# An FFT layer with two MLPs on one core: the first eight steps in written order, GpSimd kept to the squares' low parts

## The chip, the cores and the metric

The kernel runs on one core of a Trainium2 chip. The time is device microseconds of one execution, the median of 3 runs. Below, TensorE is the matmul engine (PE in the profile, PEld its weight loads), VectorE is DVE, ScalarE is ACT, GpSimd is POOL, and SyncE (SP) issues the DMAs.

## The reference

```python
X = np.fft.fft(x, axis=1)            # x is 2 x 3008 x 256
X = np.fft.fft(X, axis=2)
x = X.real.reshape(6016, 256)
h = x @ moe_w_in;  r = np.maximum(h, 0.0);  x = (r * r) @ moe_w_out     # 256 -> 2048 -> 256
h = x @ moe2_w_in; g = h / (1 + np.exp(-1.702 * h)); out = g @ moe2_w_out
```

All inputs are float32.

## The kernel before

Every float32 operand of a large matmul is split into a high part, rounded to the narrower type fp32r, and a low part, the rest; a product is three matmuls (high by high, high by low, low by high). A split costs a cast on ScalarE and a subtraction on another engine. The MLP weights come in as 64-bit words and are narrowed first: passes over 128x1024 that clamp, shift, mask, or and add (`narrow`, L162 to L187); then, for the first matrix, a sum and a difference (L207, L208), the cast (L210) and the subtraction of the low part (L78, the helper `sub`). `widen` yields these passes one by one for a weight group, named (mlp, kind, g); a step's f is the number of a slice of 128 of the 2048 hidden columns, and group g holds slices 4g to 4g+3.

The run has three stretches.

- The start: the first batch's three tiles of x (q = 0, 1, 2) are folded (`fold`: sums and differences of 128x512 and 128x1024, L281 to L293), multiplied by the feature table (`part`, L317, written to `zc` and `zs`), and summed over positions (`halves`, L361) into block (0, 0). The Nyquist terms come from a small table x128 (`fold_nyquist`, L255 to L262).
- 128 steps. Step i takes block j and slice f: `front1` is 6 matmuls into a PSUM tile pair `psa` (L462 to L464), of which there are two; VectorE makes three passes from it (L805, L807, L808: p, then the two halves of h); ScalarE relu, square and cast to the high part `gh` (L814, L815, L817); the low part `gl` is a subtraction (L78) made one step later, on GpSimd, or on VectorE in the steps of `VSTEPS`. `back` is 12 matmuls of step i - 4 (L477) into `psb`. A block's steps use weight group 0, later ones groups 1, 2, 3; step 20 is the first with group 2.
- 48 units of the second MLP (from about 480 us), in an order written by hand.

Other work of the steps (narrowing the other weights, the other blocks of batch 0, batch 1's folds) is background: `PLAN` names for each job the step where it begins, its passes per step, and the step by which it must be done; `background(i)` runs them after each step's own code. Outside the hand-written part a scheduler with its own costs and priorities sets each engine's order; from step 18 (`THROTTLE`) on, a step's background may not be issued ahead of the step's last VectorE and ScalarE instruction.

Of the kernel before, what the change touches and what calls it, by code (L numbers as in the profile page):

```python
# [16 lines left out]
P = 128  # L17
# [35 lines left out]
NP2 = 512
# [12 lines left out]
def spectral_two_mlps_kernel(  # L66
# [78 lines left out]
    x128_t = small.tile([P, 6, 8], F32, name="x128_t")  # L145
    nc.sync.dma_start(x128_t, x128)
# [3 lines left out]
    w1n_raw = small.tile([P, 32], U32, name="w1n_raw")  # L150
    nc.sync.dma_start(w1n_raw, w1n.bitcast(U32))
# [70 lines left out]
    def widen_in(g, ue, dests, then=None):  # L222
# [9 lines left out]
        for o, x, y, op in ((s3, a11, a21, ALU.subtract), (a21, a21, a22, ALU.add), (s2, a21, a11, ALU.subtract),  # L232
                            (s4, a12, s2, ALU.subtract)):
            yield lambda: G.tensor_tensor(out=o, in0=x, in1=y, op=op)
        for r in range(2):
# [7 lines left out]
            yield lambda: [sub(G, l, x, o) for o, l, x in parts]  # L243
# [22 lines left out]
    V.memset(still, 0.0)  # L266

    def keep_busy(o, k):

        for _ in range(k):  # L270
            last = T.matmul(o, lhsT=still, rhs=still, start=True, stop=True, skip_group_check=True)
        return last


    def fold(q, then=None):
        b, c = divmod(q, NC)
# [12 lines left out]
        gv = g.rearrange("p r (i j) s -> p r i j s", j=2)  # L289
        u = xt[:, 1, 0:4].rearrange("p (r j) s -> p r j s", r=2)  # L290
# [3 lines left out]
        if b == 0:  # L294

            slots = [[(u, 0, 0), (u, 1, 0)], [(u, 0, 0), (u, 1, 1)], *([(gv[:, :, j], 0, 0), (gv[:, :, j], 1, 1)] for j in range(2))]
        else:
# [3 lines left out]
            slots = [[(fu, 0, 0)], [(fu, 1, 0)], [(fv, 0, 0)], [(fv, 1, 0)]]  # L301
        if then:
            then()
        if c == 0:
            zc[b] = zp.tile([P, NC, 4, 130], F32, tag="zc", name="zc")
            zs[b] = zp.tile([P, NC, 4, P], F32, tag="zs", name="zs")

        def part(par):

            ps = ps_b() if b == 0 and par else ps_a()  # L310
            cols = slice(0, 130) if par == 0 else slice(130, 258)
            if par == 0 and q in WARM:
                keep_busy(ps[:, 0, 384:512], WARM[q])
            for s in range(4):
                o = ps[:, s // 2, (s % 2) * 130:(s % 2) * 130 + 130] if par == 0 else ps[:, 0, s * P:(s + 1) * P]
                for i, (v, j, minus) in enumerate(slots[s]):
                    T.matmul(o, lhsT=v[:, par, j], rhs=dft[:, minus, cols],  # L317
                             start=(i == 0 and (s % 2 == 0 if par == 0 else s == 0)), stop=(i == len(slots[s]) - 1),
                             skip_group_check=True)
            return ps  # L320

        def even():
            pc = part(0)
            for s in range(4 if q < 2 else 0):
# [769 lines left out]
```

## Time and profile before

| what | value |
|---|---|
| median of 3 runs | 976.22 us (975.21 to 976.83) |
| the profiled execution | 974.99 us |
| its span, first to last instruction | 973.2 us |
| mean granted TensorE clock | 0.998 of full |

The span is 1.8 us shorter than the execution's own time. Busy times of an engine are the union of its instructions; an engine off the path may be idle without cost.

### The profile page before, as it was taken

Reading aid. Unit: us, or ns where it says so; the run is one execution under the profiler, and the core shown is the slowest. Engines: PE = TensorE matmul, PEld = TensorE weight load, DVE = VectorE, ACT = ScalarE, POOL = GpSimd, SP = SyncE. Lnnn points to the kernel's source line nnn. Section 1 sums busy time; section 2 is a strip of 40 time slices with the busy share of each in tenths; the row PEclk is TensorE's granted clock in tenths of the full one; section 3 lists DMA queues with packets and bytes.
Section 4 is the critical chain, followed back from the end, with each engine's and each line's share of the span. In section 5 each row is a group of like instructions: output and inputs, shape, how many; then the busy total and the mean of one; then the engine's idle time right before and its main releaser. Section 6 shows DMA issues by size and latency. Waiting matters only on the chain.

```text
span 973.2 us, 12586 instructions
## 1 busy us (share of the span) xinstructions
PE 954.7 (98%) x4872; PEld 852.9 (88%) x4872; DVE 699.6 (72%) x870; ACT 599.6 (62%) x700; POOL 329.3 (34%) x203
## 2 busy tenths in 40 slices
PE   9899999999999999999999999999999999999998
PEld 9579989898999799999888888888888888888996
DVE  6995798985879688996689855566575476556653
ACT  3589878765676678778785644554455354445442
POOL 5358677633585457756403220020002002000000
PEclk9999999999999999999999999999999999999999
DMA  7541232311011001100131020010011002000001
GB/s 303 208 148 64 76 133 93 137 35 57 9 67 44 33 1 47 67 6 33 51 112 44 1 87 0 1 65 22 1 44 43 1 1 82 1 1 10 34 1 39
DMA packets 21899, 53.58 MB, mean 55 GB/s; under 512 B 3280, under 2 KB 15184, under 8 KB 19152
## 3 DMA queue, kind: packets, MB, share of 16 engines
q1 hardware_dynamic: 21840, 52.79, 15.4%
q8 instruction: 38, 0.62, 0.3%
q14 instruction: 21, 0.17, 0.1%
HBM read 37.36 MB, written 15.42 MB: 54 GB/s over the span
## 4 chain that ended last, share of the span: by engine, by line
PE 76%; DVE 5%; ACT 3%; issue 1%; DVEq 0%; ACTq 0%
PE psb L872 26%; PE psc L856 23%; PE psb L477 17%; PE psa L462 3%; PE psa L464 3%; PE psa L463 3%; PE psa L361 1%; ACT h L815 1%; ACT h L814 1%; ACT gh L817 1%; DVE h L807 1%; DVE p L805 0%; DVE h L808 0%; PE psa L317 0%; DVE ue L185 0%
## 5 line engine op out<-in xcount | busy, mean ns | idle before, releaser
L78 POOL TENSOR_TENSOR gl<-h,gh 128x752 fp32r<-128x752 f32 (+1 forms) x118 | 223.2, 1897 | 152.5 <-ACT gh L817 108.6
L477 PE MATMUL psb<-gh,w 128*128 128x376 f32 (+1 forms) x1024 | 237.3, 335 | 0.2 <-ACT h L814 0.2
L477 PEld LDWEIGHTS psb<-gh,w 128*128 128x128 f32 x1024 | 182.6, 188 | 0.7 <-ACT h L814 0.4
L872 PE MATMUL psb<-gh,w 128*128 128x512 f32 (+1 forms) x576 | 163.7, 386 | 0.0
L936 DVE TENSOR_TENSOR g<-u,psc 128x1024 f32<-128x1024 f32 (+1 forms) x48 | 57.6, 1201 | 115.4 <-PE psc L856 115.4
L814 ACT ACTIVATE h<-h 128x752 f32<-128x752 f32 (+1 forms) x114 | 94.8, 833 | 58.1 <-DVE h L808 48.0
L477 PE MATMUL psb<-gl,w 128*128 128x376 f32 (+1 forms) x512 | 130.1, 335 | 0.0
L938 ACT ACTIVATE g<-g 128x1536 f32<-128x1536 f32 (+1 forms) x48 | 70.4, 1467 | 95.1 <-DVE g L936 95.1
L872 PEld LDWEIGHTS psb<-gh,w 128*128 128x128 f32 x576 | 108.1, 188 | 20.6
L817 ACT CAST gh<-h 128x752 fp32r<-128x752 f32 (+1 forms) x128 | 105.1, 822 | 31.8 <-DVE h L812 28.5
L78 DVE TENSOR_TENSOR gl<-g,gh 128x2048 fp32r<-128x2048 f32 (+1 forms) x48 | 109.5, 2282 | 1.2 <-ACT gh L913 1.2
L638 POOL TENSOR_TENSOR ue<-raw 128x512 f32<-128x512 f32 (+1 forms) x10 | 21.5, 2165 | 255.0 <-DMA raw<-ydram 173.6
L805 DVE SCALAR_TENSOR_TENSOR p<-n,w1n_t,psa 128x376 f32<-128x376 f32 (+1 forms) x128 | 76.5, 600 | 43.3 <-PE psa L464 43.1
L815 ACT ACTIVATE h<-h 128x752 f32<-128x752 f32 (+1 forms) x114 | 95.2, 836 | 3.1
L462 PE MATMUL psa<-eo,w 128*128 128x376 f32 (+1 forms) x256 | 88.1, 345 | 5.0 <-DVE h L808 2.7
L477 PEld LDWEIGHTS psb<-gl,w 128*128 128x128 f32 x512 | 92.6, 188 | 0.0
L913 ACT CAST gh<-g 128x2048 fp32r<-128x2048 f32 (+1 forms) x48 | 90.3, 1881 | 0.1
L872 PE MATMUL psb<-gl,w 128*128 128x512 f32 (+1 forms) x288 | 87.7, 386 | 0.0
L463 PE MATMUL psa<-eo,w 128*128 128x376 f32 (+1 forms) x256 | 85.8, 335 | 0.0
L464 PE MATMUL psa<-eo,w 128*128 128x376 f32 (+1 forms) x256 | 85.6, 334 | 0.0
L807 DVE TENSOR_TENSOR h<-p,psa 128x376 f32<-128x376 f32 (+1 forms) x128 | 69.7, 545 | 13.9 <-POOL gl L78 1.0
L935 ACT ACTIVATE g<-psc 128x512 f32<-128x512 f32 (+1 forms) x48 | 28.3, 590 | 76.0 <-PE psc L856 76.0
(151 smaller groups left out, 1551.1 us busy)
## 6 DMA issues: line engine op xcount, KB each, us to landing
ydram<-o SPq DMA_DIRECT2D x17, 376.0 KB, 2.9
xt<-in_x SPq DMA_DIRECT2D x5, 1024.0 KB, 7.0
out<-o SPq DMA_DIRECT2D x10, 512.0 KB, 2.6
cst<-in_dfts SPq DMA_DIRECT2D x8, 570.0 KB, 5.2
raw<-in_w1i SPq DMA_DIRECT2D x4, 1024.0 KB, 4.9
raw<-in_w1o SPq DMA_DIRECT2D x4, 1024.0 KB, 5.8
raw<-in_w2i SPq DMA_DIRECT2D x4, 1024.0 KB, 4.9
raw<-in_w2o SPq DMA_DIRECT2D x4, 1024.0 KB, 4.9
```

The lines of the kernel that those rows point to most:

```text
L78: eng.tensor_tensor(out=o, in0=a, in1=f32(b), op=ALU.subtract)
L462: T.matmul(o, lhsT=w[:, 0, fs], rhs=t[:, par, 0, 0:wd], start=True, stop=False)
L463: T.matmul(o, lhsT=w[:, 0, fs], rhs=t[:, par, 1, 0:wd], start=False, stop=False)
L464: T.matmul(o, lhsT=w[:, 1, fs], rhs=t[:, par, 0, 0:wd], start=False, stop=True)
L477: T.matmul(acc[j][ec][:, s, 0:wd], lhsT=w[:, hl, e0:e0 + P], rhs=(gh, gl)[gi][:, s, 0:wd], start=(first and hl == 0 and gi == 0), stop=(la ...
L807: V.tensor_tensor(out=h[:, 0, 0:wd], in0=p[:, 0:wd], in1=ps[:, 1, 0:wd], op=ALU.add)
L814: A.activation(out=hv, in_=hv, func=AF.Relu)
L815: A.activation(out=hv, in_=hv, func=AF.Square)
L817: last_a = A.copy(gh[:, :, 0:wd], hv)
L856: T.matmul(bank, lhsT=w[:, hl, slot * P:(slot + 1) * P], rhs=x[:, yl, 0:wd], start=(first and hl == 0 and yl == 0), stop=(hl == 1), skip_g ...
L872: T.matmul(o[:, s, 0:wd], lhsT=w[:, hl, e0:e0 + P], rhs=g[:, 2 * i + s, 0:wd], start=(f == 0 and hl == 0 and g is gh), stop=(f == 15 and h ...
L913: A.copy(gh, gs[u - 1])
```

## The change

The start is no longer left to the scheduler: from the first load to the end of step 7 the order of every engine is as the code is written (`HAND = 8`). In detail:

- VectorE makes all folds and the Nyquist terms, which stand first in its order; GpSimd made half of the differences and the Nyquist terms. The loads of x128 and of the small weight table stand ahead of the feature table's.
- The first tile needs one fold pass fewer and 12 matmuls a part where it had 8. 24 warm-up matmuls on zeros stand ahead of it where there were 36; the groups of 3 and of 5 in the first steps are gone.
- Block (0, 1)'s sums stand ahead of step 0's front; they stood between step 0's front matmuls. Their evacuation and the narrowing of (0, 1, 0) are set into places of steps 0 to 5.
- The narrowing of the other weights of the first MLP (`conv`) begins at step 5; it began at step 3, free of the throttle until step 18. The throttle now begins at step 8.
- All low parts of weights and of blocks, and the sums of the second MLP's first groups, go to VectorE; `VSTEPS` is empty, so that GpSimd makes every `gl`.
- From step 8 on `gl` of step i is made in step i + 2, and waits for the last of VectorE's narrowing passes in the background of step i + 1; the first VectorE pass of a step stands behind that last pass in VectorE's order.

```diff
 PLAN = {
-    "out0": (0, 12, 3), "even01": (0, 1, 4), "odd0": (1, 1, 48), "conv": (3, 1.2, 36),
+    "odd0": (6, 1, 48), "conv": (5, 1.2, 36),
-WARM = {0: 36, 2: 4, "first": 3, "second": 5}
-THROTTLE = 18
+WARM = {0: 24, 2: 2}
+HAND = 8
+THROTTLE = HAND
...
-VSTEPS = {44, 45, 50, 69, 71, 79, 82, 99, 101, 109}
+VSTEPS = set()
-EOG = {1, 2, 3}
+EOG = set()
...
     load_x(0)
+    x128_t = small.tile([P, 6, 8], F32, name="x128_t")
+    nc.sync.dma_start(x128_t, x128)
+    w1n_raw = small.tile([P, 32], U32, name="w1n_raw")
+    nc.sync.dma_start(w1n_raw, w1n.bitcast(U32))
     dft = zp.tile([P, 2, 258], F32, tag="dft", name="dft")
...
-            yield lambda: G.tensor_tensor(out=o, in0=x, in1=y, op=op)
+            yield lambda: V.tensor_tensor(out=o, in0=x, in1=y, op=op)
...
+        z_tiles(0)
+        fold_nyquist()
+        run(fold_rows(0))
+        z_even(0, part(0, 0))
+        run(fold_rows(1))
+        z_odd(0, part(0, 1))
+        w_abs()
+        z_even(1, part(1, 0))
+        run(fold_rows(2))
+        w_low()
+        z_odd(1, part(1, 1))
...
+        put(0, "front", copy, o_low, adds)
+        put(0, "V", high)
+        put(1, "front", nyquist)
+        put(1, "V", n_copy1, low)
+        put(1, "A", n_adds1, o_shift)
+        put(2, "front", next_of(odd))
+        put(2, "V", next_of(odd), o_or, o_add)
+        put(2, "A", lambda: load_w(0, 1, 1), out_high)
+        put(3, "front", next_of(odd))
...
+    def behind_tail(x, sync):
+        kind = mybir.DependencyClass.Sync if sync else mybir.DependencyClass.NoSync
+        tc.add_manual_dep(x.ins, tail[0].name, mybir.DependencyInfo(kind, mybir.DependencyReason.DATA), reason="tail")
...
     def background(i):
+        tail[0] = last_v.ins
...
-            if not run(entry[2], int((i + 1) * entry[1]) - int(i * entry[1])):
+            before = len(traced())
+            more = run(entry[2], int((i + 1) * entry[1]) - int(i * entry[1]))
+            if entry[0] in NARROW:
+                of_v = [x for x in traced()[before:] if x.engine == last_v.ins.engine]
+                if of_v:
+                    tail[0] = of_v[-1]
...
+        if i > THROTTLE:
+            behind_tail(first_v, False)
...
-        if pend:
-            low_part(*pend)
-        pend = (i, (j, f), h, gh)
+        do_early(i, "A")
+        pend.append((i, (j, f), h, gh))
+        if len(pend) > (1 if i < THROTTLE else 2):
+            low = low_part(*pend.pop(0))
+            if low is not None and i > THROTTLE:
+                behind_tail(low, True)
```

Three places show what moves. VectorE at the start of the program, before (`t`, `xt` are fold tiles, `ne`, `nu` and `nyq` the Nyquist terms):

```order
L266 MEMSET still 128x128
L283 TENSOR_TENSOR t<-xt 128x512 x2
L287 TENSOR_TENSOR xt<-t 128x512
L288 TENSOR_TENSOR xt<-t 128x512
L293 TENSOR_TENSOR xt<-xt 128x512
L281 TENSOR_TENSOR t<-xt 128x512
```

The same place of VectorE in the changed kernel:

```order
L265 MEMSET still 128x128
L255 TENSOR_TENSOR ne<-x_t 128x24
L257 TENSOR_TENSOR nyq<-ne 128x6x2
L258 TENSOR_TENSOR nu<-ne 128x12
L259 TENSOR_TENSOR nyq<-nu 128x6
L260 TENSOR_TENSOR nyq<-nu 128x6
L261 TENSOR_SCALAR nyq<-nyq 128x24
L281 TENSOR_TENSOR t<-xt 128x512
L282 TENSOR_TENSOR t<-xt 128x512
L281 TENSOR_TENSOR t<-xt 128x512
L282 TENSOR_TENSOR t<-xt 128x512
L286 TENSOR_TENSOR xt<-t 128x512
```

Six Nyquist passes and two differences have come in ahead of the first tile's last fold.

TensorE around step 0's front before (L361 with `cst` are the block sums, L462 to L464 the front):

```order
L361 MATMUL psa<-cst,zs 128x188 x2
L462 MATMUL psa<-eo,w 128x378 x2
L361 MATMUL psa<-cst,zc 128x188 x2
L361 MATMUL psa<-cst,zs 128x188 x2
L463 MATMUL psa<-eo,w 128x378
L464 MATMUL psa<-eo,w 128x378
```

And in the changed kernel (the front is L480 to L482):

```order
L369 MATMUL psb<-cst,zc 128x189 x4
L369 MATMUL psb<-cst,zc 128x188 x4
L369 MATMUL psb<-cst,zs 128x188 x4
L480 MATMUL psa<-eo,w 128x378
L481 MATMUL psa<-eo,w 128x378
L482 MATMUL psa<-eo,w 128x378
```

Block (0, 1)'s sums now stand whole ahead of the first front matmul.

The low part of weight group (0, 0, 2) before, on GpSimd (here w_894; h_517, h_558, h_594 and h_626 are the squares of steps 4, 5, 6 and 7):

```order
L78 TENSOR_TENSOR gl_567<-h_517,gh_524 128x2x376
L207 TENSOR_TENSOR ue_809<-ue_809 128x512
L78 TENSOR_TENSOR gl_603<-h_558,gh_565 128x2x376
L78 TENSOR_TENSOR gl_642<-h_594,gh_601 128x2x376
L78 TENSOR_TENSOR w_894<-ue_809,w_894 128x1024
L78 TENSOR_TENSOR gl_662<-h_626,gh_640 128x2x376
```

The same group in the changed kernel, on VectorE (w_972; p_996 is of step 18, p_1028 of step 19, p_1058 of step 20; L755 is a copy out of a block's sums):

```order
L208 SCALAR_TENSOR_TENSOR ue_868<-ue_868,mask_122 128x512
L959 SCALAR_TENSOR_TENSOR p_996<-n_397,w1n_t_123,psa_975 128x376
L963 TENSOR_TENSOR h_995<-p_996,psa_976 128x376
L964 TENSOR_TENSOR h_995<-p_996,psa_976 128x376
L959 SCALAR_TENSOR_TENSOR p_1028<-n_397,w1n_t_123,psa_1007 128x376
L963 TENSOR_TENSOR h_1027<-p_1028,psa_1008 128x376
L964 TENSOR_TENSOR h_1027<-p_1028,psa_1008 128x376
L755 COPY o_1036<-psb_796 128x2x376
L80 TENSOR_TENSOR w_972<-ue_868,w_972 128x1024
L959 SCALAR_TENSOR_TENSOR p_1058<-n_397,w1n_t_123,psa_1049 128x376
```

It has moved from between the low parts of steps 6 and 7 to just ahead of step 20's first pass, and step 20 is the first that uses it.

## Rows read from the trace of the kernel before

**Rows 1.** The page, part 1: busy time by engine.
```profile
PE 954.7 (98%) x4872; PEld 852.9 (88%) x4872; DVE 699.6 (72%) x870; ACT 599.6 (62%) x700; POOL 329.3 (34%) x203
```
**Rows 2.** Busy time by stretch: length, engines (instructions), clock, DMA share, GB/s.
```profile
31.60:79.30 47.70, 43.12 (x211) 34.29 (x211) 43.33 (x62) 36.86 (x49) 28.55 (x14) 0.96 0.44 162
79.30:110.00 30.70, 30.70 (x180) 30.70 (x179) 19.86 (x33) 26.22 (x34) 20.14 (x12) 1.00 0.11 39
110.00:185.20 75.20, 70.56 (x399) 67.40 (x399) 67.96 (x99) 59.95 (x75) 51.49 (x28) 1.00 0.36 119
185.20:480.00 294.80, 294.22 (x1695) 285.76 (x1694) 234.48 (x346) 214.27 (x272) 172.75 (x103) 1.00 0.11 38
```
**Rows 3.** Busy time by stretch: the clock's fall and return, and a steady stretch.
```profile
47.50:50.20 2.70, 0.29 (x1) 0.00 (x0) 2.70 (x5) 0.84 (x1) 2.70 (x2) 1.00 0.69 291
50.20:53.60 3.40, 3.27 (x6) 1.67 (x8) 3.40 (x5) 1.75 (x3) 0.75 (x1) 0.50 0.01 2
...
250.00:300.00 50.00, 50.00 (x291) 50.00 (x291) 42.12 (x60) 37.31 (x47) 33.44 (x22) 1.00 0.11 37
```
**Rows 4.** Timeline of TensorE's start: start us, us, instruction, [idle before <-releaser].
```profile
1.03 10.58 PE L271 MATMUL psa<-still 128*128 128x128 f32 x72 [1.03 <-DVE still L266]
11.46 1.95 PE L317 MATMUL psa<-dft,xt 128*128 128x130 f32 x16
13.24 1.95 PE L317 MATMUL psb<-dft,xt 128*128 128x128 f32 x16
...
24.34 1.33 PE L361 MATMUL psa<-cst,zc 128*128 128x189 f32 x8
...
31.57 0.61 PE L462 MATMUL psa<-eo,w 128*128 128x378 f32 x2
...
39.09 5.34 PE L361 MATMUL psa<-cst,zc 128*128 128x188 f32 x20
...
50.33 4.55 PE L361 MATMUL psa<-cst,zs 128*128 128x376 f32 x12 [2.54 <-DVE ue L420]
```
**Rows 5.** Timeline of TensorE: the first matmul of step 11, and of step 42.
```profile
79.35 0.33 PE L462 MATMUL psa<-eo,w 128*128 128x376 f32 x1
...
185.24 0.33 PE L462 MATMUL psa<-eo,w 128*128 128x376 f32 x1
```
**Rows 6.** Waits of TensorE, 110 to 185 us: us in total, times, longest.
```profile
PE psa L462 <- DVE h L808: 2.0, 5, 1.0
```
**Rows 7.** Lines L805, L176 and L78: ns min/median/max, first and last start.
```profile
L805 DVE SCALAR_TENSOR_TENSOR p<-n,w1n_t,psa x128: 590/599/609, 34.6 to 472.0; 128x376 f32<-128x376 f32 x96, 128x378 f32<-128x378 f32 x32
...
L176 DVE TENSOR_SCALAR ue<-ue x14: 678/695/1924, 21.3 to 512.4; 128x1024 uint32<-128x1024 uint32 x14
...
L78 POOL TENSOR_TENSOR gl<-h,gh x118: 1782/1830/2630, 41.9 to 476.6; 128x752 fp32r<-128x752 f32 x89, 128x756 fp32r<-128x756 f32 x29
```
**Rows 8.** Timeline of SP: the issue of x128's load.
```profile
2.73 0.43 SPq L146 DMA_DIRECT2D x_t<-in_x  x1
```
**Rows 9.** DMA issues: the same load: count, KB, us to landing.
```profile
x_t<-in_x SPq DMA_DIRECT2D x1, 24.0 KB, 5.1
```
**Rows 10.** Timeline of VectorE: folds, a weight's low part, step 16's last two passes.
```profile
6.75 0.69 DVE L283 TENSOR_TENSOR t<-xt 128x512 f32<-128x512 f32 x1 [1.43 <-DMA xt<-in_x]
...
19.92 0.69 DVE L293 TENSOR_TENSOR xt<-xt 128x512 f32<-128x512 f32 x1
...
30.43 1.22 DVE L78 TENSOR_TENSOR w<-ue,w 128x1024 fp32r<-128x1024 f32 x1
...
96.25 0.55 DVE L807 TENSOR_TENSOR h<-p,psa 128x376 f32<-128x376 f32 x1
96.71 0.54 DVE L808 TENSOR_TENSOR h<-p,psa 128x376 f32<-128x376 f32 x1
```
**Rows 11.** Timeline of ScalarE: a weight's cast, a weight's first pass, step 16's relu.
```profile
27.37 1.04 ACT L210 CAST w<-ue 128x1024 fp32r<-128x1024 f32 x1 [2.25 <-DVE ue L208]
...
30.75 1.16 ACT L171 ACTIVATE ue<-raw 128x1024 f32<-128x1024 f32 x1
...
97.28 0.83 ACT L814 ACTIVATE h<-h 128x752 f32<-128x752 f32 x1 [0.45 <-DVE h L808]
```

More of the change, by code (lines that the diff above doesn't have):

```diff
@@ L266, in spectral_two_mlps_kernel, with fold_rows @@
     V.memset(still, 0.0)
+    A.activation(out=w1n_t[:, 0, 0:1], in_=still[:, 0:1], func=AF.Abs)
     def keep_busy(o, k):
         for _ in range(k):
[L271 to L276, printed above, removed]
+            T.matmul(o, lhsT=still, rhs=still, start=True, stop=True, skip_group_check=True)
+    def fold_rows(q):
         xt = xq.pop(q)
         t = xp.tile([P, 2, 8, P], F32, tag="t", name="t", bufs=1)
+        eng = V
         for a in XPARTS[q]:
             yield lambda: (
-                *(e.tensor_tensor(out=t[:, 1, i], in0=xt[:, 0, i], in1=xt[:, 1, i], op=ALU.subtract)
-                  for e, i in (((G, slice(0, 4)), (V, slice(4, 8))) if q in (1, 2) else ((G, a),))),
+                eng.tensor_tensor(out=t[:, 1, a], in0=xt[:, 0, a], in1=xt[:, 1, a], op=ALU.subtract),
                 V.tensor_tensor(out=t[:, 0, a], in0=xt[:, 0, a], in1=xt[:, 1, a], op=ALU.add),
@@ L304, in fold @@
         if c == 0:
[L305 to L324, printed above, removed]
[L325 to L344 removed]
+            z_tiles(b)
+        for par, z in ((0, z_even), (1, z_odd)):
             for _ in range(2 * b):
                 yield lambda: None
[L347 removed]
+            yield lambda: z(q, part(q, par))
     eo, e128 = {}, {}
@@ L429, in nyquist @@
             e128[b, kb] = t
-        yield lambda: sums(0)
-        yield lambda: sums(1)
-        yield lambda: split_eo(b, 2, e2)
+        if b:
+            for par in range(2):
+                yield lambda: (sums(par), leaves(par))
+            yield lambda: split_eo(b, 2, e2)
+        else:
+            for job, par in ((sums, 0), (leaves, 0), (sums, 1), (leaves, 1)):
+                yield lambda: job(par)
+            t = eo[b, 2] = ep.tile([P, 2, 2, NP], F32R, tag="eo", name="eo")
+            yield lambda: A.copy(t[:, :, 0, 0:wd], e2)
+            yield lambda: sub(V, t[:, :, 1, 0:wd], e2, t[:, :, 0, 0:wd])
         yield from [lambda: None] * b
@@ L456, in front1 @@
         pq = ps_a()
-        if at_step[0] == 0 and j == 0:
-            keep_busy(pq[:, 0, 384:512], WARM["first"])
         for par in range(2):
@@ L605, in store @@
             nc.sync.dma_start(y[:, ec, :, 0:wd], o)
-    pend = None
+    pend = []
     n = len(steps)
@@ L789, in spectral_two_mlps_kernel @@
         ps = front1(j, f)
-        if i == 1:
-            o = ps_b()[:, 0, 0:128]
-            for _ in range(WARM["second"]):
-                tc.keep_in_program_order(keep_busy(o, 1))
+        do_early(i, "front")
         done = steps[i - LAG][1:] if i >= LAG else None
```

227 lines of the change are left out of this document (171 added, 56 removed).

## The prediction

> **What bounds the kernel now.** I read the page's busy times first: TensorE is busy for 98% of the span, so only its idle and slow stretches can be won back [rows 1]. The table of stretches says where they are. From 185.2 to 480 us TensorE is busy for 294.22 of 294.80 us: nothing is to be had there, whatever the other engines do [rows 2]. A steady step is 18 matmuls of 376 columns; 291 of them in 50.00 us are 0.172 us each, 3.10 us a step [rows 3]. Two stretches fall short: 31.6 to 79.3 (43.12 of 47.70 us busy, clock 0.96) and 110 to 185.2 (70.56 of 75.20) [rows 2].
>
> The timeline of TensorE gives the first its size. Step 0's front begins at 31.57 us, step 11's at 79.35 [rows 4, 5]: 47.8 us. The work between is 11 fronts of 6 matmuls and 7 backs of 12, 150 x 0.172 = 25.8 us; block (0, 1)'s sums, 16 records at the 1.33 per eight of block (0, 0), 2.7; its Nyquist sums, 8 records, 1.4; the odd blocks' sums, 32 records at 5.34/20, 8.5; a selection of two matmuls, 0.4 [rows 4]. Sum 38.8 us, so 9.0 are lost, to waits (the longest 2.54 us, for VectorE's L420) and to a clock of 0.50 (its level of 1.2 GHz) for the 3.40 us after that wait [rows 3, 4].
>
> For the second, take step 11 to step 42, 79.35 to 185.24: 105.9 us [rows 5]. 31 steps are 96.1; batch 1's first tile (16 records at 0.111, from the 1.78 us between two parts of 16) and a selection are 2.2 [rows 4]. So 7.6 us are lost; the wait named most often is for the step's third pass on VectorE [rows 6].
>
> Why VectorE is late there: a step's three passes read PSUM and keep their time (590 to 609 ns for the first), but L176, which reads SBUF, takes 678 ns at best and 1924 at worst, beside GpSimd's subtractions of 1.83 us [rows 7].
>
> **The change, part by part.** I sum against the profiled execution, 974.99 us. Two passes of 0.55 us start 0.46 apart [rows 10]; I take 0.08 of overlap off each pass.
>
> *To step 0.* VectorE now begins with the Nyquist terms, so it waits for x128. Before, that load was issued at 2.73 us and landed 5.1 later, at 7.8 [rows 8, 9]; now it goes out third, behind x's two halves, the second of which had landed by 6.75 [rows 10]. I take 7.0 (bounds 6.0 to 7.8). The feature table goes out behind two small loads; it is needed only at 12 us: 0. Six small passes: 0.2 each, 1.2 us (not in the trace on this scale; between 0.1 and the 0.55 of larger ones). Six passes of 512 columns at 0.61: the first tile is ready at 12.0, against TensorE's first real matmul at 11.46 [rows 4]. Tiles 1 and 2 cost two long passes (1.2) and three short each, 4.3 us: 16.3 and 20.6. Before, the last fold pass ended at 20.61 with GpSimd's help [rows 10]: folding on VectorE alone costs nothing, as the two engines had slowed each other.
>
> TensorE: 72 warm-up records took until 11.46, about 21 of them at half speed [rows 4]. The new 48 end near 8.8. It then idles for some 3.3 us; the one such wait in the trace, 2.7 us, was followed by the low clock [rows 3]. If so, the next 3.4 us run at half speed and 1.6 us are lost. Then 48 records for tile 0 (5.4), 32 each for tiles 1 and 2 (3.6, and 0.4 of warm-up): 25.0 us at full clock. Block (0, 0)'s sums 2.7, its Nyquist sums 1.4, block (0, 1)'s sums 3.3 (2.7 to 3.9): step 0's front begins at 32.4 at full clock, at 34.0 with the low one, against 31.57. VectorE and ScalarE are ready by 31.1: after the sums a copy (0.5), the weight's cast (1.04), the block's cast (0.8), two low parts (1.2 and 0.9) [rows 10, 11].
>
> *Step 0 to step 11.* Block (0, 1)'s sums now lie ahead, so TensorE has 38.8 - 2.7 = 36.1 us of work. VectorE, from step 0's first pass to step 8's: eight steps of 1.44 us; four passes of 1.14, three of 0.61, four of 0.46, two low parts and a copy of 0.86 each and 0.5 of Nyquist terms, 11.3; and some 2.5 of waits for ScalarE: 25.3 us. TensorE's own work to step 8 is 26.8, so VectorE follows it. Step 11 comes at 32.4 + 36.1 = 68.5, or 70.1 with the low clock, against 79.35: a gain of 10.9 or 9.3. I take 10.0.
>
> *Step 11 to step 42.* Narrowing that ran before step 11 is moved into steps 8 to 33. VectorE's load there is 1.44 us for the step, about 1.15 for narrowing, 0.1 for copies: 2.7 of 3.10. ScalarE's is three passes of 0.83, or 0.75 back to back, and 3.3 us (two first passes, one cast) per weight, 0.7 a step: 2.9 to 3.2 [rows 11]. Both fit, hardly. But a weight's clamp (behind ScalarE's first pass) and its low part (behind the cast) stand ahead of the next step's first pass, so each of ten such places can hold VectorE up. Followed through the order, the two around steps 9 to 13 cost TensorE 2.6 us. Step 20 needs group (0, 0, 2), whose low part now stands just ahead of that step's pass: after step 19's last pass come a relu and a cast (0.83 each), the weight's cast (1.04) and its low part (1.22) [rows 10, 11], and TensorE has two backs, 4.1 us, to fill in: 1.0. The other places: 2.0. Steps 36 to 42, with batch 1's folds: 2.0. Sum 7.6, as much as before: 0. Bounds: 2.5 lost (79.3 to 110 was full [rows 2]) to 15, a gain of 5 or a loss of 7.4.
>
> A rule weighed: beside GpSimd's 1.83 us a VectorE pass grew from 0.68 to 1.92 us [rows 7]. The Trainium skill (SBUF — State Buffer, "SBUF: two separate sides") says that the two engines share one port pair, which one of them holds for a whole instruction. By that the new place of `gl`, beside a step's three passes, isn't free: they last 1.44 us, so the narrowing pass behind them still waits 0.4. Over 25 steps that is 10 us of VectorE, within its slack of 0.4 a step; if all of it fell on the path, the gain would be gone.
>
> *`gl` two steps late.* It starts beside VectorE's first pass of step i + 2 and takes 1.83 us; its matmuls come behind step i + 4's front, 7.2 us after step i + 2's front begins. It is late only if VectorE lags by over 4.6 us; the two `psa` pairs stop TensorE earlier, at 3.7. Queued behind a waiting `gl` on GpSimd are only other `gl`. Cost 0 (-0.5 to 2).
>
> *Rest.* VectorE takes on some 21 us of low parts and folds and gives back ten `gl`. From 185 to 480 us it is busy for 234.48 of 294.80 [rows 2], and the passes lose their collisions: 0.
>
> Sum: 974.99 - 10.0 = 965.0. The median of the runs is 1.23 us above the profiled execution, so I predict 966.2.
>
> **Rivals.**
>
> 1. *The clock stays up and narrowing runs smoothly.* For it: VectorE is freed of the collisions that stretch L176. Against: the idle 3.3 us. Gain 10.9 + 5 = 15.9: 960.3.
>
> 2. *VectorE and ScalarE become the bound in steps 8 to 33* (slower). Place: VectorE's order, where a clamp or low part that waits for ScalarE stands ahead of the next step's p. Where ScalarE lags a full step, such a step lasts relu, square and cast 2.5, a first pass 1.16, two narrowing passes 1.3 and the step's own 1.44: 6.4 us, 3.3 more than TensorE's. Ten places: 33 us. It decides from 1.76 us a place, where 10.0 + 7.6 us are used up. At 3.3 each: 966.2 + 33 - 7.6 = 991.6. For it: ScalarE's 2.9 to 3.2 of 3.10 us. Against: two `psa` pairs let VectorE lag by 3.7 us.
>
> 3. *The start's gain is given back.* TensorE, earlier, meets the narrowing undone: steps 11 to 42 lose 15 us. 966.2 + 7.4 = 973.6.
>
> The Trainium skill (TensorE: Matmul & The Clock Gate, "Part 1") says that an idle array falls to its lower clock by itself. Rows 3 agree; that speaks against rival 1's full gain.
>
> **How the numbers follow.** Forecast (gain 5 to 14) 0.65: 962 to 971. Rival 1 (over 14) 0.10. Rival 3 (gain 2 to 5) 0.10. Within 2 us, about the 0.2% that a measurement of this kernel can tell from no change, 0.06. Rival 2 0.09. Faster 0.85, same 0.06, slower 0.09. The range leaves out part of rival 1 and what lies above a gain of 2: 958.5 to 974.0.
>
> **What would show it.** VectorE's first pass at about 7 us and tile 2's last at 20.6; TensorE's clock at 0.50 after 12 us or not; step 0's front at 32.4 to 34.0, step 11's at 68.5 to 70.1, step 42's 9 to 11 us before 185.24; L176 near 0.7 us. Wrong would be VectorE waiting for ScalarE by over 1.5 us at most of the ten places, TensorE waiting for `gl`, or a stretch from 185 us on that isn't full.

## The result, and the profile after

| | kernel before | changed kernel |
|---|---|---|
| median | 976.53 us (4 runs) | 990.1 us (4 runs, 987.9 to 991.68) |
| ratio, 95% interval | | 1.0137 [1.0118, 1.0155] |
| the profiled execution | 974.99 us | 987.9 us |

The change is slower by 1.4%; the forecast was 966.2 us, 23.9 less. The table of stretches of the changed kernel, with the bounds of [rows 2]; a column is busy time with the count of instructions, then TensorE's granted clock:

```profile
core 0: us, PE busy (x) PEld busy (x) DVE busy (x) ACT busy (x) POOL busy (x), PEclk, DMA share, GB/s
31.60:79.30 47.70, 44.86 (x231) 38.80 (x230) 38.13 (x60) 38.50 (x50) 18.61 (x10) 0.96 0.37 130
79.30:110.00 30.70, 26.84 (x139) 25.03 (x138) 24.51 (x37) 25.80 (x33) 14.57 (x9) 0.94 0.27 94
110.00:185.20 75.20, 64.89 (x338) 59.89 (x338) 58.45 (x87) 53.98 (x66) 36.03 (x19) 0.95 0.26 88
185.20:480.00 294.80, 292.33 (x1684) 283.43 (x1683) 223.06 (x366) 215.13 (x272) 169.42 (x93) 1.00 0.13 44
```

The stretch from 79.3 to 110 us, full before, now lacks 3.9 us, the next one 10.3 where it lacked 4.6. A table by time mixes steps, since the steps have moved. TensorE's timeline gives the fronts of steps 0, 11 and 42 (start, duration, line):

```profile
30.75 0.44 PE L480 MATMUL psa<-eo,w 128*128 128x378 f32 x1
...
67.83 0.34 PE L480 MATMUL psa<-eo,w 128*128 128x376 f32 x1
...
197.27 0.34 PE L480 MATMUL psa<-eo,w 128*128 128x376 f32 x1
```

Against 31.57, 79.35 and 185.24 [rows 4, 5], step 0 is 0.8 us earlier, step 11 is 11.5 earlier and step 42 is 12.0 later. From there on the distance stays between 12 and 14 us. So the start does what was forecast, and steps 11 to 42 lose 23.5 us that the forecast put at 0.

The same steps side by side, first the kernel before, then the changed one:

```profile
0.00:79.35 79.35, 72.53 (x425) 61.06 (x426) 67.26 (x98) 50.10 (x79) 42.35 (x34) 0.98 0.57 212
79.35:185.24 105.89, 101.25 (x577) 98.09 (x577) 87.86 (x130) 86.15 (x108) 71.62 (x40) 1.00 0.29 96
```

```profile
0.00:67.83 67.83, 64.40 (x397) 56.93 (x398) 55.70 (x92) 44.90 (x79) 17.90 (x18) 1.00 0.59 217
67.83:197.27 129.44, 111.41 (x577) 103.02 (x577) 100.58 (x146) 94.60 (x115) 59.24 (x35) 0.95 0.27 93
```

Up to step 11 VectorE does 11.56 us less, and step 11 comes 11.52 us earlier: much of what the start gained is work put off. Five weights had been through VectorE's narrowing by step 11, now three have. It isn't all of it, though: with five weights narrowed again (v3_early, below) the new start still has step 11 3.6 us early, and the old start with only three (y3_before_late) wins just 2.1. Between steps 11 and 42 VectorE does 12.7 us more: some 3.6 are narrowing (five weights in place of three, each in less time), 5.4 the weights' low parts and sums and 3.0 the folds that came from GpSimd. TensorE has the same 577 matmul records there (98.3 us of work by the prediction's count), so VectorE's 100.6 alone is over what TensorE needs. And VectorE waits. The waits of the changed kernel between 68 and 200 us (total, times, longest):

```profile
POOL gl L980 <- DVE w L80: 21.7, 6, 4.7
POOL gl L980 <- DVE ue L176: 16.0, 4, 5.0
DVE w L80 <- ACT w L210: 11.7, 5, 3.6
DVE ue L175 <- ACT ue L171: 10.3, 4, 3.7
PEld psb L495 <- POOL gl L980: 9.2, 10, 2.9
...
PEld psa L480 <- DVE p L959: 6.3, 7, 2.2
```

VectorE stands nine times, 22.0 us in all, behind ScalarE's first pass of a weight (L171) or its cast (L210). Busy and waiting make 122.6 of the 129.4 us: the path runs along VectorE's order, through its own passes and its waits. The same sum holds in all fifteen kernels below, this one included, that have every weight's low part on VectorE: steps 11 to 42 take 107 to 138 us there, 2 to 9 us more than VectorE is busy and waits for ScalarE. One such place, in step 11, from the timelines of ScalarE, VectorE and TensorE (the bracket is the idle time before and what ended it):

```profile
67.63 0.83 ACT L971 ACTIVATE h<-h 128x752 f32<-128x752 f32 x1 [0.35 <-DVE h L964]
68.50 0.83 ACT L972 ACTIVATE h<-h 128x752 f32<-128x752 f32 x1
69.36 0.82 ACT L974 CAST gh<-h 128x752 fp32r<-128x752 f32 x1
70.09 1.04 ACT L210 CAST w<-ue 128x1024 fp32r<-128x1024 f32 x1
...
67.00 0.54 DVE L964 TENSOR_TENSOR h<-p,psa 128x376 f32<-128x376 f32 x1
71.16 1.23 DVE L80 TENSOR_TENSOR w<-ue,w 128x1024 fp32r<-128x1024 f32 x1 [3.62 <-ACT w L210]
72.30 0.60 DVE L959 SCALAR_TENSOR_TENSOR p<-n,w1n_t,psa 128x376 f32<-128x376 f32 x1
...
73.05 0.41 PE L480 MATMUL psa<-eo,w 128*128 128x376 f32 x1 [1.98 <-DVE p L959]
```

ScalarE makes the step's relu, square and cast and only then casts the weight; VectorE does nothing from 67.54 to 71.16, because the weight's low part stands next in its order, ahead of step 10's first pass, whose front was done at 65.9; TensorE, out of free `psa` pairs, stands for 1.98 us, and 1.7 us later its clock falls.

The clock adds to it: it is at 0.50 four times, after pauses of TensorE, where [rows 3] has one such stretch:

```profile
74.80:78.10 3.30, 3.30 (x12) 2.97 (x11) 1.66 (x3) 3.30 (x6) 1.30 (x1) 0.50 0.50 190
105.50:108.80 3.30, 3.30 (x11) 3.30 (x12) 1.07 (x2) 3.30 (x5) 0.32 (x1) 0.50 0.63 233
156.70:160.00 3.30, 3.30 (x11) 3.30 (x12) 3.17 (x5) 2.09 (x3) 0.96 (x1) 0.50 0.45 109
170.40:173.70 3.30, 3.30 (x11) 3.30 (x12) 3.17 (x4) 2.35 (x3) 2.04 (x1) 0.50 0.51 214
```

Each lasts 3.4 us, so they cost 4 x 1.7 = 6.8 us. TensorE's idle time between steps 11 and 42 has grown from 4.6 to 18.0 us (13.4). Together 20.2 of the 23.5. The other 3.3 lie at the edges of the pauses: by the start times of its records, the last matmul before a pause and the first behind it take 0.29 us more than two in a row (0.17 each), and there are 21 pauses of over 0.1 us where there were 10; that makes 3.4.

### The profile page after: what moved, and what is told of

Its sections match the earlier page's. It is cut to its first block, busy times and chain, and to the rows that moved or that the text cites. A ratio compares the mean times of both kernels' runs of the same rounds, so it can differ in the third digit from the quotient of the medians.

```text
span 986.1 us, 12560 instructions
## 1 busy us (share of the span) xinstructions
PE 957.4 (97%) x4844; PEld 854.2 (87%) x4844; DVE 683.6 (69%) x895; ACT 607.1 (62%) x710; POOL 292.3 (30%) x172
## 4 chain that ended last, share of the span: by engine, by line
PE 78%; DVE 4%; issue 0%; ACT 0%; POOL 0%; DVEq 0%; POOLq 0%; ACTq 0%
PE psb L1035 26%; PE psc L1019 22%; PE psb L495 19%; PE psa L480 3%; PE psa L482 3%; PE psa L481 3%; PE psa L369 2%; DVE t L282 1%; DVE o L753 0%; DVE p L959 0%; DVE h L964 0%; DVE t L281 0%; DVE h L963 0%; DVE yc L80 0%; DVE g L1099 0%
## 5 line engine op out<-in xcount | busy, mean ns | idle before, releaser
L980 POOL TENSOR_TENSOR gl<-h,gh 128x752 fp32r<-128x752 f32 (+1 forms) x128 | 244.7, 1915 | 215.3 <-DVE h L964 45.0
L495 PE MATMUL psb<-gh,w 128*128 128x376 f32 (+1 forms) x1024 | 240.4, 338 | 3.6 <-ACT o L755 2.3
L495 PE MATMUL psb<-gl,w 128*128 128x376 f32 (+1 forms) x512 | 133.4, 342 | 6.2 <-POOL gl L980 6.1
L1035 PEld LDWEIGHTS psb<-gh,w 128*128 128x128 f32 x576 | 108.1, 188 | 20.5
L80 DVE TENSOR_TENSOR gl<-g,gh 128x2048 fp32r<-128x2048 f32 (+1 forms) x48 | 109.5, 2282 | 1.2 <-ACT gh L1076 1.2
L480 PE MATMUL psa<-eo,w 128*128 128x376 f32 (+1 forms) x256 | 89.4, 349 | 8.5 <-DVE p L959 7.4
L482 PE MATMUL psa<-eo,w 128*128 128x376 f32 (+1 forms) x256 | 85.9, 337 | 0.0
```

The costliest lines, as they stand in the source:

```text
L80: eng.tensor_tensor(out=o, in0=a, in1=f32(b), op=ALU.subtract)
L480: T.matmul(o, lhsT=w[:, 0, fs], rhs=t[:, par, 0, 0:wd], start=True, stop=False)
L482: T.matmul(o, lhsT=w[:, 1, fs], rhs=t[:, par, 0, 0:wd], start=False, stop=True)
L495: T.matmul(acc[j][ec][:, s, 0:wd], lhsT=w[:, hl, e0:e0 + P], rhs=(gh, gl)[gi][:, s, 0:wd], start=(first and hl == 0 and gi == 0), stop=(la ...
L980: low = eng.tensor_tensor(out=gl[:, :, 0:pw], in0=h[:, :, 0:pw], in1=f32(gh[:, :, 0:pw]), op=ALU.subtract)
L1035: T.matmul(o[:, s, 0:wd], lhsT=w[:, hl, e0:e0 + P], rhs=g[:, 2 * i + s, 0:wd], start=(f == 0 and hl == 0 and g is gh), stop=(f == 15 and h ...
```

## The experiments

Eighteen kernels ran, in five groups of runs, each with runs of the kernel before beside it (their medians were 975.8 to 976.2 us). The table has the median, the ratio to before with its interval, and from the one profiled execution how much later than before a step's front begins (us; minus is earlier). "Lost" is step 42 minus step 11. The start by itself comes out up to 2 us apart from one profile to the next (see the part on the prediction), so a difference of 2 us in the columns of steps 8 and 11 says nothing of an edit.

| run | median | ratio | step 8 | step 11 | step 42 | lost |
|---|---|---|---|---|---|---|
| changed kernel | 990.1 | 1.0137 [1.0118, 1.0155] | -11.2 | -11.5 | +12.0 | 23.5 |
| x1_no_tail | 1010.82 | 1.0358 [1.0343, 1.0374] | | -9.2 | +22.7 | 31.8 |
| x3_free18 | 981.45 | 1.0061 [1.0044, 1.0077] | | -5.4 | +4.8 | 10.1 |
| x4_start_only | 985.45 | 1.0103 [1.0086, 1.0119] | | -4.6 | +9.5 | 14.1 |
| x5_gap | 980.87 | 1.0049 [1.0034, 1.0064] | | -11.2 | +3.2 | 14.4 |
| y1_gap18 | 977.26 | 1.0007 [0.9997, 1.0017] | -9.6 | -4.7 | +2.0 | 6.7 |
| y2_rate16 | 997.61 | 1.0221 [1.0206, 1.0237] | -9.8 | -5.9 | +22.0 | 27.9 |
| y4_gap18_dense | 981.79 | 1.0061 [1.0045, 1.0078] | -9.9 | -3.0 | +5.1 | 8.1 |
| y3_before_late | 992.26 | 1.0169 [1.0153, 1.0185] | -1.6 | -2.1 | +14.6 | 16.7 |
| y6_before_t8 | 983.32 | 1.0079 [1.0064, 1.0094] | +2.0 | +1.5 | +7.6 | 6.1 |
| z1_folds | 980.39 | 1.0047 [1.0032, 1.0062] | -9.5 | -4.0 | -2.8 | 1.2 |
| z2_free12 | 978.75 | 1.0026 [1.0016, 1.0036] | -9.1 | -9.5 | +3.8 | 13.3 |
| z3_both | 981.63 | 1.0059 [1.0041, 1.0076] | -8.7 | -9.1 | -0.6 | 8.5 |
| w1_fold34 | 975.95 | 0.9994 [0.9985, 1.0004] | -11.7 | -6.4 | -1.5 | 4.9 |
| w2_tie5 | 976.88 | 1.0004 [0.9994, 1.0013] | -11.4 | -6.5 | +0.2 | 6.7 |
| w3_both | 976.13 | 0.9995 [0.9986, 1.0005] | -9.6 | -4.7 | +0.6 | 5.4 |
| x6_g_lows | 988.07 | 1.0123 [1.0106, 1.0140] | -8.9 | -9.2 | +11.3 | 20.5 |
| v2_no_narrow | 974.04 | 0.9972 [0.9962, 0.9982] | -9.8 | -9.4 | -2.5 | 6.9 |
| v3_early | 980.27 | 1.0046 [1.0031, 1.0061] | -4.2 | -3.6 | +3.3 | 6.9 |

Three theories of the 23.5 us were tried. Theory A: VectorE stands in order behind ScalarE's narrowing passes. Theory B: `gl`, tied behind VectorE's narrowing, comes late. Theory C: narrowing is begun later, so more of it is left for steps 11 to 36.

**The tie of `gl` (theory B): x1_no_tail.**

```diff
-            if low is not None and i > THROTTLE:
-                behind_tail(low, True)
```

> The changed kernel without the wait of a square's low part for VectorE's last narrowing pass; everything else, the two steps' delay too, stays. Theory A (VectorE stands behind ScalarE: in steps 8 to 36 a clamp or a weight's low part that waits for ScalarE stands ahead of the next step's p; 22.0 us of such waits from 68 to 200 us): the waits stay, TensorE waits for VectorE in place of GpSimd, 985 to 990. Theory B (the tie itself: GpSimd waits 46 us for VectorE's tails there and TensorE 9.2 us for gl): those 9.2 us and the clock's falls behind them go, 974 to 980.

It came out 20.7 us slower, outside both ranges; half of that comes only behind step 42 (step 127 is 35.8 us later than before, where the changed kernel has 13.0). VectorE's passes with the tie, then without it, between 68 and 200 us (count, total, mean ns):

```profile
L185 DVE SCALAR_TENSOR_TENSOR ue<-raw,ue 128x1024 uint32<-128x1024 uint32 x5 | 7.9, 1574 | 0.0
L80 DVE TENSOR_TENSOR w<-ue,w 128x1024 fp32r<-128x1024 f32 x6 | 7.3, 1223 | 11.7 <-ACT w L210 11.7
L175 DVE TENSOR_SCALAR ue<-ue 128x1024 f32<-128x1024 f32 x5 | 3.5, 692 | 10.3 <-ACT ue L171 10.3
```

```profile
L80 DVE TENSOR_TENSOR w<-ue,w 128x1024 fp32r<-128x1024 f32 x6 | 11.7, 1950 | 11.8 <-ACT w L210 11.8
L185 DVE SCALAR_TENSOR_TENSOR ue<-raw,ue 128x1024 uint32<-128x1024 uint32 x5 | 9.9, 1990 | 0.0
L175 DVE TENSOR_SCALAR ue<-ue 128x1024 f32<-128x1024 f32 x5 | 6.3, 1269 | 9.7 <-ACT ue L171 9.7
```

Theory B falls: VectorE, which carries the path here, is spared 9.2 us of longer passes in these three lines by the tie. Pass by pass, the L80 and L185 that meet no GpSimd instruction take 1.21 and 1.22 us, those that meet a `gl` 1.91 to 2.86. VectorE's waits for ScalarE are the same with and without the tie (22.0 and 21.5).

**The order behind the step's own passes (theory A): x3_free18, x5_gap, y1_gap18, y2_rate16, y4_gap18_dense.**

```diff
# x3_free18
-            if THROTTLE <= i < n:
+            if 18 <= i < n:
# x5_gap (with "conv": (5, 1.6, 36), which keeps the low parts' steps)
-        for k in first + ((1,) if kind else (4, 1, 2) if mlp else (2, 1)):
+        for n_, k in enumerate(first + ((1,) if kind else (4, 1, 2) if mlp else (2, 1))):
             yield lambda: run(gen, k)
+            if n_ == 0:
+                yield lambda: None
+        yield lambda: None
         yield lambda: run(gen)
# y1_gap18: both. y2_rate16: only "conv": (5, 1.6, 36). y4_gap18_dense: y1_gap18 with (5, 2.1, 36)
```

> The changed kernel with the throttle on background work beginning at step 18, as before, in place of step 8; the ties stay. Theory A: ScalarE's first passes and casts can again be placed ahead of a step's own passes until step 18, so about half of the 22 us of VectorE's waits go: 972 to 980. Theory B: the ties stay, 986 to 991.

> The changed kernel with one empty place between a weight's first passes on ScalarE and its clamp on VectorE, and one between its cast and its low part (the first MLP's groups 1 to 3; 1.6 places a step in place of 1.2, so that they end at the same step). Theory A: VectorE's 22 us of waits for ScalarE shrink to under 8, and the time with them, 970 to 980. Theory B: no change, 986 to 992.

> The changed kernel with both single edits at once: an empty place between a weight's first passes on ScalarE and VectorE's clamp, and between the cast and the low part (x5_gap, 980.87), and the order of passes left to the scheduler up to step 18 instead of step 8 (x3_free18, 981.45). If VectorE's standing in order behind ScalarE is the cause (theory A) both edits act on different places (free order on steps 8 to 17, the empty places on all), and the gains of 9.2 and 8.7 us add in large part: 971 to 975. If both only buy the same thing, the weights of steps 12 to 20 in time (theory C), one of them is enough: 979 to 982.

> The changed kernel with the narrowing dealt out at 1.6 places a step instead of 1.2 and no empty places: the weights' low parts then stand in steps 7, 10, 14, 17, 21 and 24 instead of 9, 14, 19, 23, 28 and 32. If late weights are the cause (theory C) it gains as much as x5_gap did: 978 to 983. If VectorE behind ScalarE is the cause (theory A), there are as many such places, only closer together, so that ScalarE has less time to catch up in between: 990 to 998.

> As y1_gap18, with the narrowing at 2.1 places a step instead of 1.6: low parts in steps 7, 8, 14, 18, 21 and 25. Theory A: as y1_gap18 or up to 5 us slower, since an empty place is then less often a step of its own. Theory C: up to 6 us faster than y1_gap18, 966 to 974, as the weights of steps 20 to 36 come earlier and batch 1's folds (from step 31) meet no narrowing.

Each of the first two wins back about 9 us and ends just above theory A's range (to 980 in both). VectorE's waits for ScalarE in x5_gap, same stretch:

```profile
DVE w L80 <- ACT w L210: 8.8, 5, 2.2
DVE ue L175 <- ACT ue L171: 6.4, 3, 2.3
```

15.2 us where there were 22.0 and theory A expected under 8. Together (y1_gap18) they bring 12.8 and not 17.9: between the two theories. y2_rate16, whose weights come earlier without empty places, is 7.5 us slower than the changed kernel, with VectorE waiting 25.7 us for ScalarE between steps 11 and 42: earlier weights alone don't help, which speaks against theory C in its form "the weights are late". y4_gap18_dense is 4.5 slower than y1_gap18, as theory A allowed and theory C did not.

**The same order in the kernel before: y3_before_late, y6_before_t8.**

```diff
-    "conv": (3, 1.2, 36),
+    "conv": (5, 1.2, 36),        # y3_before_late only
-THROTTLE = 18
+THROTTLE = 8                     # both
```

> The kernel before with one thing of the change: the narrowing of the later groups begins at step 5 instead of 3 and each step's share stands behind the step's own passes from step 8 instead of 18; start, engines of low parts and folds, and gl as before. Theory C (what was narrowed before step 11 is missing later): slower than before by 8 to 16 us, 984 to 992. Theory A: the places where VectorE stands behind ScalarE are made by the same order, so 984 to 992 too, with VectorE waiting for ScalarE over 2 us a place. If the loss comes from the other parts (low parts on VectorE, the ties, gl late): within 3 us of before.

> The kernel before with one number changed: each step's share of the narrowing stands behind the step's own passes from step 8 instead of 18; the narrowing still begins at step 3. With the later beginning too (y3_before_late) it took 992.26, 16 us more than before. If the order behind the step's own passes costs (theory A), most of the 16 us are in it: 985 to 990. If the late beginning costs (theory C): 976 to 980.

These two lines, with nothing else of the change, cost 16.05 us, at the upper end of theory C's range; the throttle alone costs 7.5, between the two theories again. The later beginning alone did not run. The table shows where the 16 us are: 16.7 between steps 11 and 42. Up to step 11 VectorE does 9.1 us less than in the kernel before (58.12 us against 67.26) and step 11 gains only 2.1 by it; behind it VectorE is busy 102.26 of 122.64 us, against 87.86 before:

```profile
0.00:77.20 77.20, 70.03 (x424) 60.06 (x425) 58.12 (x88) 43.93 (x72) 37.63 (x33) 1.00 0.51 191
77.20:199.84 122.64, 105.02 (x577) 98.70 (x577) 102.26 (x140) 92.12 (x115) 77.03 (x40) 0.99 0.30 99
```

But its waits for ScalarE are 1.3 us in all, so theory A's half of the expectation was wrong: no VectorE waiting over 2 us a place. VectorE waits for TensorE instead (12.0 us), and TensorE for VectorE and, 4.8 us at its weight loads, for two low parts on GpSimd. I take VectorE's load and these low parts for the cost here; no run separates them. So VectorE's waits for ScalarE are a price of the changed kernel's own order, and narrowing put off costs in both orders.

**GpSimd's share and the start alone: x6_g_lows, x4_start_only.**

```diff
# x6_g_lows: LOW, VSTEPS, EOG, LOWE as before, and
-            yield lambda: V.tensor_tensor(out=o, in0=x, in1=y, op=op)
+            yield lambda: G.tensor_tensor(out=o, in0=x, in1=y, op=op)
...
-        eng = V
+        eng = G if q >= NC else V
...
-            yield lambda: [sub(V, l, x, o) for o, l, x in parts]
+            yield lambda: [sub(G, l, x, o) for o, l, x in parts]
# x4_start_only: these, without the two ties, gl one step late, and throttle from 18
```

> The changed kernel with GpSimd's share of low parts, folds and ten gl steps as in the kernel before; order, ties and gl two steps late stay. If VectorE's standing behind ScalarE's cast is what costs (theory A), the weights whose low part goes back to GpSimd no longer hold VectorE up: 980 to 986. If GpSimd's passes beside VectorE cost as much again (1.8 us each, and VectorE's pass beside them twice as long): 988 to 996.

> The written start (steps 0 to 7) alone: from step 8 on the throttle at 18, low parts one step late, no ties, and GpSimd's and VectorE's shares of low parts, folds and sums as in the kernel before. Both theories: the start's 11.5 us (step 11's front at 67.83 against 79.35 us) are kept and the rest is as before, 963 to 969. If it is slower than 972, the start itself, or narrowing that begins at step 5, costs the later steps their time.

Low parts back on GpSimd: 988.07, 2 us less; VectorE has fewer waits for the cast (5.6 us) but more for the first pass (16.6). VectorE's busy time between steps 11 and 42 falls to 92.3 us, under what TensorE needs, and 20.5 us are lost all the same; TensorE's weight loads now wait 6.5 us for GpSimd's low parts. So where the low parts are made hardly matters, and a load under TensorE's need is not enough while the waits stay. x4_start_only missed its expectation by 16 us or more: without the ties, with `gl` and the shares as before and VectorE waiting only 0.5 us for ScalarE, the new start still loses 14.1 us by step 42, with VectorE busy 96.7 us there. That speaks for theory C and against A as the whole cause; what makes up the 14.1 is open. Against x3_free18, the change's other parts are worth 4 us.

**The places one by one: z1_folds, z2_free12, z3_both, w1_fold34, w2_tie5, w3_both, v3_early.** All start from y1_gap18.

```diff
-"fold3": (31, 1.5, 40), "fold4": (38, 1.5, 46), "fold5": (45, 1.5, 52)
+"fold3": (35, 2, 41), "fold4": (41, 2, 47), "fold5": (47, 2, 52)   # z1_folds
+"fold3": (34, 2, 40)                                               # w1_fold34: only this one
+            if THROTTLE <= i < 12 or 18 <= i < n:                  # z2_free12
+            if low is not None and i > 5:                          # w2_tie5, the tie of gl
+"conv": (2, 1.6, 36)                                               # v3_early: w1_fold34 with it
# z3_both: z1 and z2; w3_both: w1 and w2
```

> As y1_gap18, with the folds of batch 1 put behind the last weight's narrowing (from steps 35, 41 and 47 at two places a step, instead of 31, 38 and 45 at 1.5). In y1_gap18 TensorE waits 3.43 us at 150.8 us for a gl that stands behind a step in which VectorE narrows and folds, and the clock falls after it (1.7 us). If that meeting is the cause, both go: 972 to 974. If VectorE's total of steps 30 to 50 is too much wherever it stands: 976 to 979.

> As y1_gap18, with the order left to the scheduler in steps 12 to 17 only and not in 8 to 11. In y1_gap18 TensorE waits 3.08 us at 60.4 us for a first pass that VectorE's narrowing (1.9 to 2.4 us a pass beside gl) stands ahead of, and the clock falls after it (1.7 us); in the changed kernel, whose narrowing stands in order there, it doesn't. If that is so: 972 to 974. If the steps 8 to 11 in order only put it off: 976 to 980.

> z1_folds and z2_free12 at once. The two places are 90 us apart, so their gains should add: 967 to 970, faster than the kernel before by 6 to 9 us. If the start's gain can't be kept because the narrowing put off has to be made later at TensorE's cost (theory C in its strict form): not under 975.

> As y1_gap18, with only the first fold of batch 1 moved from step 31 to step 34, behind the last weight's narrowing; the other two folds stand where they stood. z1_folds removed the wait of 3.43 us at 150.8 us and its clock fall (step 42 came 4.8 us earlier than in y1_gap18) but lost 10 us behind step 44, where the later folds met batch 1's even and odd blocks. If those two folds' places are the cause of that loss: 972 to 974, and from step 44 on as y1_gap18. If the first fold's delay is: 977 to 981.

> As y1_gap18, with gl held behind VectorE's narrowing from step 6 on instead of from step 9; no engine's order changes. In y1_gap18 VectorE's passes of 1.89, 2.43 and 1.93 us at 52 to 60 us stand beside a gl (alone they take 0.69, 1.21 and 1.21), and TensorE waits 3.08 us for VectorE at 60.4 us, with a clock fall (1.7 us) after it. If the passes beside gl are the cause: 972.5 to 974.5. If gl, held back, becomes the wait itself: 976 to 980.

> w1_fold34 and w2_tie5 at once: 967.5 to 970 if both places go, which would be faster than the kernel before by 6 to 8 us; 973 to 976 if one of them does; 977 or more if neither.

> As w1_fold34 (975.95), with the narrowing begun at step 2 instead of step 5, so that low parts stand in steps 6, 10, 13, 18, 23 and 27. If the start's gain is narrowing put off and nothing else, step 11 comes later and what follows loses as much less: 974 to 979, no better than the kernel before. If the start's gain stands by itself and only the narrowing's lateness costs: 967 to 971.

None of the gains hoped for came. z1_folds loses only 1.2 us between steps 11 and 42, but 10 more by step 54; w1_fold34, which leaves the two later folds where they stood, loses 1.6 there, so their places make the difference. z2_free12 keeps step 11 at -9.5 and loses 13.3 behind it; z3_both, 981.63, adds nothing. w1_fold34 takes the place at step 33 away (step 34 at -4.9, in y1_gap18 +1.6), and gives 3.4 of it back by step 42. w2_tie5 tested nothing: the passes stayed beside `gl` (1.82, 2.35 and 1.94 us, where 1.89, 2.43 and 1.93 stood), probably since the scheduler had set them behind the tail that `gl` waits for; no row shows that. v3_early, with narrowing begun at step 2, has step 11 at -3.6 and ends 4.3 us slower than w1_fold34, above both its ranges: what was narrowed earlier cost the start its lead, but behind step 11 it lost 6.9 us where w1_fold34 loses 4.9. So theory C in its strict form (what is put off comes back, and nothing else) fails too. The best, w1_fold34, equals the kernel before. In every order that ran with all of the work in it, the start's gain is paid back.

**The work itself: v2_no_narrow.**

```diff
+        if key in RA and key[2] and key[0] == 0:
+            yield from (lambda: None for _ in range(3))
+            return
         yield lambda: V.tensor_scalar(out=uu, in0=uu, scalar1=3, ...
```

> The changed kernel without three of VectorE's passes (shift, combine, add: 0.69, 1.57 and 1.23 us) for each of the six weights narrowed from step 5 on; the clamp, ScalarE's passes, the low parts, ties and order stay. It leaves that part of the computation out. If narrowing, put off from the start into steps 11 to 36, is what takes the gain back: 966 to 972, with step 11 as in the changed kernel and step 42 about 10 us before that of the kernel before. If the waits for ScalarE alone do it, whose passes all stay: 980 to 986. If the ties or the late gl do: 987 to 990.

The run leaves that part of the work out, and is 16.1 us faster than the changed kernel, between two of the expectations. Steps 11 to 42, as a window:

```profile
69.97:182.79 112.82, 103.76 (x578) 99.13 (x578) 86.14 (x131) 90.54 (x112) 59.63 (x34) 0.98 0.32 106
```

VectorE is busy as long as in the kernel before (86.1), but still waits 14.9 and 9.7 us for ScalarE; busy and waiting are 110.7 of 112.8. So 16.6 of the 23.5 us lost go with three of VectorE's narrowing passes, and 6.9 stay. VectorE's waits for ScalarE are no shorter (24.6 us, before 22.0), so they cost most where VectorE has no slack to take them up.

## Why the prediction was wrong

*The start: right.* Step 11 was forecast at 68.5 to 70.1 us and came at 67.83; in the other runs whose narrowing is as late (x1, x5, x6) at 68.1 to 70.2. VectorE's first pass stands at 6.88 (forecast 7.0), tile 2 is folded by 20.33 (forecast 20.6), step 0 begins at 30.75 (32.4 at full clock, so the sum to step 0 was 1.6 us too long). The low clock at the start was priced well too (1.6 us), though the profiled execution had none: of 17 profiles with the new start, 11 show the clock at 0.50 from 11.0 to 12.7 us on, behind a pause of TensorE's matmuls of 2.6 to 3.3 us, and step 0 at 32.5 to 33.2; six don't, behind pauses of 1.8 to 2.4 us, with step 0 at 30.8 to 31.6. The changed kernel (no fall), then y1_gap18 (a fall), each with TensorE's first real matmul and a window behind it:

```profile
11.01 1.72 PE L320 MATMUL psa<-dft,xt 128*128 128x130 f32 x13 [1.77 <-DVE xt L286]
12.60:15.90 3.30, 3.30 (x32) 3.30 (x31) 3.23 (x5) 1.83 (x8) 0.00 (x0) 1.00 1.00 408
```

```profile
11.48 0.71 PE L323 MATMUL psa<-dft,xt 128*128 128x130 f32 x4 [2.61 <-DVE xt L289]
12.60:15.90 3.30, 3.30 (x17) 3.30 (x16) 3.23 (x5) 0.94 (x4) 0.00 (x0) 0.50 1.00 408
```

The same kernel can come out either way, it seems: v2_no_narrow's ten runs fall into seven of 973.9 to 974.3 us, with a mean clock of 0.996, and three of 971.6 to 972.0, with 0.998. The profiled run of the changed kernel (987.9) is the fastest of its four.

*Step 11 to step 42, "Sum 7.6, as much as before: 0": wrong by 23.5 us.* The stretch lost 129.44 - 98.3 = 31.1 us. By the prediction's parts, at 3.10 us a step (in brackets the loss that it put there): steps 11 to 14 lost 5.1 (2.6 around steps 9 to 13), 14 to 18 1.1, 18 to 22 5.2 (1.0), 22 to 32 10.9 and 32 to 36 7.8 (2.0 for all other places together), 36 to 42 1.1 (2.0). Two things failed. First, the load: 2.7 us of VectorE a step is 83.7 for 31 steps, and batch 1's folds take VectorE 17.2 more in this stretch (14.3 in the kernel before, which left two of their passes to GpSimd). The sum, 100.9, is near what was measured (100.58), but it was never set against the 98.3 that TensorE needs. The folds were given 2.0 us of loss and no place in the load. Second, a mean load was taken as if the two engines could fill each other's gaps: in order, VectorE's 22.0 us of waiting for ScalarE adds to its 100.6. The two `psa` pairs, which the prediction trusted to let VectorE lag by 3.7 us, did not cover even the first hold: 3.62 us in step 11 stopped TensorE for 1.98. How the 23.5 us divide between load and waits the runs show only from one side: without three of the narrowing passes 6.9 stay, with all the waits (v2_no_narrow); with VectorE's load under TensorE's need by moving other work, 20.5 stay (x6_g_lows).

*Rival 2 is what came:* its 33 us lost in the stretch and 991.6 us stand against 31.1 and 990.1. Its place was right, VectorE's order; its price was luck (nine waits of 2.4 us, not ten of 3.3; the load and the clock made up the rest). Its sign came too: eight of the nine waits are longer than 1.5 us. I gave it 0.09, though the forecast says of VectorE's and ScalarE's load: "Both fit, hardly." That sentence, and the warning behind it that each of ten places can hold VectorE up, should have made it the likeliest case. Rival 3, TensorE meeting the narrowing undone, was at work beside it: it fits what x4_start_only and y3_before_late lose, but its 15 us were less than half of the 31.1. The Trainium skill (PSUM — Partial Sum Buffer, "Engine vs sequencer instructions") states that VectorE's and ScalarE's queues are strictly first in, first out; the rows of step 11 show it: L80 waits 3.62 us with the next first pass behind it.

*`gl` two steps late, cost 0: wrong.* TensorE's weight loads wait for it ten times, 9.2 us, and its matmuls stand 6.1 of them. The forecast let `gl` start beside VectorE's first pass of step i + 2, but it is tied to the last narrowing pass, and where that waits or is long, `gl` waits with it. At the last weight and batch 1's first fold:

```profile
161.88 2.85 DVE L282 TENSOR_TENSOR t<-xt 128x1024 f32<-128x1024 f32 x1
...
166.69 1.21 DVE L80 TENSOR_TENSOR w<-ue,w 128x1024 fp32r<-128x1024 f32 x1
...
168.07 4.36 POOL L980 TENSOR_TENSOR gl<-h,gh 128x756 fp32r<-128x756 f32 x2 [4.42 <-DVE w L80]
...
170.25 0.97 PE L495 MATMUL psb<-gl,w 128*128 128x378 f32 x2 [2.61 <-POOL gl L980]
```

Still, the tie is worth 20.7 us in this order, and from step 11 on L175 and L176 take 0.69 us, as forecast for L176 [rows 7]. The rule weighed there (the Trainium skill, SBUF — State Buffer, "SBUF: two separate sides": one engine holds the shared ports for a whole instruction) agrees with x1_no_tail, whose L80 and L185 take 1.95 and 1.99 us on the mean, where they take 1.22 and 1.57 with the tie.

*The rest, 0:* from step 42 to step 127 the changed kernel loses 0.9 us more. Right.

## What to carry to other kernels

Work that a start leaves out is not saved until the stretch that takes it has room: add up each engine's busy time from the step where the gain shows to the step where the work is done, all moved work included, and set it against what the bounding engine needs there. That is a warning and not the whole sum: where two engines hand work to each other in order, waits add to the load, and x6_g_lows lost 20.5 us with VectorE's load 6 us under TensorE's need. A mean load near the step's time leaves no room for such waits. A hold that looks like a new wait (the tie of `gl`) can pay for itself by sparing the engine that has become the bound, so take it away by experiment before blaming it.

## What the runs showed of the hardware

TensorE's clock fell to 0.50 (1.2 of its 2.4 GHz) after a pause of 2.0 us at 71 to 73 us in the changed kernel, yet pauses of up to 2.4 us at the start left it at 1.00 in six of 17 profiles: the same start can come out 2 us apart. VectorE's two fold passes over 128x1024 took 1.55 and 2.85 us at 160 to 165 us, beside two `gl` in a row on GpSimd; at the start, with GpSimd idle, L282 took 1.22. In x1_no_tail L80 took 1.21 us with no `gl` beside it and 2.01 to 2.37 where it met one.
